# Decay attention with two expert layers: loads of 128 rows, and another order of the attention steps

## The chip, the cores and the metric

The kernel runs on 1 core of one Trainium2 chip. The metric is the device time of one execution in microseconds (us); smaller is better. Times are medians of several executions; one execution was also recorded by the profiler, and all rows below come from that one.

## The reference

Three parts follow each other. The first is a linear attention with a decay for each channel, over 4 batches, 8 heads, 768 steps and 48 channels a head:

```
for t in range(S):
    state = alpha[:, :, t, :, None] * state + einsum('bhd,bhe->bhde', k[:, :, t], v[:, :, t])
    y[:, :, t] = einsum('bhd,bhde->bhe', q[:, :, t], state)
```

Its output, as 3072 rows of 384, goes through a first expert layer (8 experts of 384 x 1024, one for each row, weighted by two gates) and a second one (8 experts, rows with a score of 0 or less skipped, the input added).

## The kernel before

The attention is worked in 24 chunks of 128 steps (`NTILE`), six for each batch. In a chunk, P is the running product of the decay; q is multiplied by P, k divided by it, and what is left is matmuls. Two heads share a tile: one on rows 0 to 47, the other on rows 64 to 111, so a tile of q, k or alpha has 112 rows (`PR`), of which rows 48 to 63 are padding. Three chunks make a half (`HB`), and a half is what a load brings; there are 8 halves. `ain`, `kin` and `qin` (alpha, k, q) have three buffers each, `vin` two.

A chunk i goes through these steps, each a function: `p_scan(i)` (DVE, L877) makes P. `p_recip(i)` (ACT, L886 and L887) makes r = 1/P as exp(-ln P). `p_q(i)` multiplies q by P (DVE, L915; ACT copies the chunk's last P into `ptots`, L919). `p_k(i)` makes the k product in three steps: t = P x r on POOL (L903; t has one buffer), then on DVE r = k x r (L904) and k2 = (2 - t) x r (L906), which corrects the reciprocal. `scores(i)` multiplies k2 by q on PE (L928), copies the result on ACT (L931) and masks it on POOL (L932, two AFFINE_SELECT). `k_back(i)` transposes k2 (PE L945, ACT L947). `state(i)` makes the state S after the chunk (PE L961 and L962, DVE L966 to L969); it reads v. `y_of(i)` makes the output (PE L980, L986; ACT L988), `x_rows(i)` turns it to rows (PE L269, ACT L274). `p_check(i)` (ACT, L893) tests alpha. Every fourth chunk closes a group of 512 tokens: `x_route` chooses experts (seven small DVE instructions, L147 to L246), `x_place` computes positions and sends the rows to memory with four indirect DMAs that POOL prepares (L218).

The order on every engine is the order in which the code issues the steps. A short written list (`lead`) starts the first chunks; then pass i of a loop calls the steps of the table `stages`, each with its lag: (p_scan, 4) in pass i is the scan of chunk i + 4. At the end of a pass come the DMAs of that pass. All of those loads go through SP's queue in that order: the halves (`load_half`), v (`load_v`), weight pieces of the first expert, and the fills, which write empty rows into the two scratch regions `scr1` (8 DMAs) and `scr2` (8 DMAs). For halves 3 to 7 `load_half` loads rows 0 to 47 and 64 to 111 with a DMA each, so that the padding stays; for the first three it loads all 112 rows. Some passes also split a weight piece into two parts (ACT L303, DVE L304).

Behind the attention come the two expert layers (`stream`), which begin with rows that the indirect DMAs of the attention's last full group but one have written.

Of the kernel before, what the change touches and what calls it, by code (L numbers as in the profile page):

```python
# [8 lines left out]
F32 = mybir.dt.float32  # L9
# [26 lines left out]
P1, G1 = 108, 4  # L36
# [8 lines left out]
FILL = 4  # L45
# [7 lines left out]
def kernel(  # L53
# [17 lines left out]
    nc = tc.nc  # L71
# [15 lines left out]
    scr1 = dp.tile([E * CAP + N1, PAY], F32, name="scr1")  # L87
# [759 lines left out]
    with ExitStack() as actx:  # L847
# [3 lines left out]
        ps1 = pool(actx, "ps1", 1, PSUM)  # L851
        NB_IN = 3
        NQ = 4
        ain = [inp.tile([128, HB, NP, C + 1], F32, name=f"ain{i}") for i in range(NB_IN)]
        kin = [inp.tile([128, HB, NP, C], F32, name=f"kin{i}") for i in range(NB_IN)]
        qin = [inp.tile([128, HB, NP, C], F32, name=f"qin{i}") for i in range(NB_IN)]
        vin = [inp.tile([128, HB, DM], F32, name=f"vin{i}") for i in range(2)]
        NHALF = 2 * B

        def load_half(h, which="akq", c0=0, c1=HB):  # L860
            s = h % NB_IN
            for r0, r1 in ((0, PR),) if h < NB_IN else ((0, 48), (64, PR)):
                for t in which:
                    dst, src = {"a": (ain[s], ad), "k": (kin[s], kd), "q": (qin[s], qd)}[t]
                    nc.sync.dma_start(out=dst[r0:r1, c0:c1], in_=src[h, r0:r1, c0:c1])

        def load_v(h):
            b, u = divmod(h, 2)
            nc.sync.dma_start(out=vin[h % 2], in_=vn[b][:, u * HB:(u + 1) * HB])

        P_t, r_t, k_t, q_t, A_t, kn_t, S_t, x_t, xt_t, sm_t, rt_t, lt_t = ({} for _ in range(12))

# [161 lines left out]
        def among(fn, i0, i1):  # L1034
            def run(i):
                if i0 <= i < i1:
                    fn(i)

            return run
# [1 line left out]
        rest = NTILE - GT * (LATE + 1)  # L1041
        x_route_0, x_place_0 = (among(fn, 0, rest) for fn in (x_route, x_place))
        x_route_1, x_place_1 = (among(fn, rest, NTILE) for fn in (x_route, x_place))
        p_q_0, p_q_1 = among(p_q, 0, NTILE - 1), among(p_q, NTILE - 1, NTILE)

        nbias = cp.tile([128, 1], F32, name="nbias")
        floor = cp.tile([128, NP, C + 1], F32, name="floor")
# [12 lines left out]
        for which, c in (("ak", 0), ("a", 1), ("q", 0), ("kq", 1), ("a", 2)):  # L1060
# [10 lines left out]
        w_cur = alloc_w(wpe, 0)  # L1071
        pieces = []
        stages = (
            (state, -1), (x_route_1, -3), (p_k, 2), (scores, 0), (k_back, 0), (x_place_0, -4), (x_place_1, -3),
            (x_route_0, -3), (p_recip, 3), (p_q_0, 2), (p_q_1, 1), (y_of, -1), (p_scan, 4), (x_rows, -2), (p_check, 0),
        )

        def constants(n):
# [2 lines left out]

        lead = (
            (p_scan, 0), (p_q, 0), (p_recip, 0), (p_scan, 1), (p_recip, 1), (p_k, 0), (p_q, 1), (scores, 0), (k_back, 0),
            (p_k, 1), (p_scan, 2), (p_recip, 2), (constants, FILL), (scores, 1), (k_back, 1),
            (p_q, 2), (p_scan, 3), (p_k, 2), (p_recip, 3), (state, 0), (y_of, 0), (scores, 2), (k_back, 2), (p_scan, 4),
        )
        for fn, i in lead:
            fn(i)
        done = lead + tuple((p_q_0, i) for fn, i in lead if fn is p_q)
        early_at = (NTILE // GT - LATE) * GT - 1 - dict(stages)[x_place_1]  # L1090
        for i in range(NTILE + 2):
            if i == early_at + 1:
                bump(ohs1, ecl1, sm_t[NTILE // GT - LATE - 1][0:1, 400:401], EARLY1)
            for fn, lag in stages:
                if 0 <= i + lag < NTILE and (fn, i + lag) not in done:
                    fn(i + lag)
                if fn is p_scan and 6 <= i < 24 and i % 3:
                    split_half(w_cur, (i - 6) // 3, i % 3 - 1, pieces[(i - 6) // 3])
            if i % HB == 1 and 2 <= (i + 2) // HB < NHALF:
                load_v((i + 2) // HB)  # L1100
            if i == early_at:
                xe = []
                for g0 in range(0, ITEMS[0][4], 2):
                    g1 = min(g0 + 2, ITEMS[0][4])
                    st = stp.tile([128, 1024], F32, name="st")
                    part = st[:, 0:(g1 - g0) * PAY].rearrange("p (g d) -> p g d", g=g1 - g0)
                    load_into(part, ITEMS[0], g0, g1)
                    xe += [part[:, g] for g in range(g1 - g0)]
            if i == 8:
                fill_region(scr2, P2, G2)  # L1110
            if i == HB:
                load_half(HB, "a")
                fill_region(scr1, P1, G1, FILL)
            if i >= HB and i % HB == 1 and i // HB + 2 < NHALF:
                load_half(i // HB + 2, "akq" if i > HB + 1 else "kq")
            if 4 <= i and i % 3 == 1 and (i - 4) // 3 < 6:
                pieces.append(load_piece(w1a, w2a, 0, (i - 4) // 3, stp))

# [102 lines left out]
def _lay_out(x):  # L1221
    import numpy as np

    q, k, v, a = (np.asarray(x[n]) for n in ("q", "k", "v", "alpha"))

    def d_major(t, pad):
        o = np.full((B, PR, NP, S), pad, t.dtype)
        r = t.reshape(B, NP, 2, S, D).transpose(2, 0, 4, 1, 3)
        o[:, 0:48] = r[0]
        o[:, 64:PR] = r[1]  # L1230
        return o

    def by_chunk(t, edge):
        o = np.zeros((2 * B, PR, HB, NP, C + edge), t.dtype)
        o[..., edge:] = t.reshape(B, PR, NP, 2, HB, C).transpose(0, 3, 1, 4, 2, 5).reshape(2 * B, PR, HB, NP, C)
        return o

    qm, km, am = d_major(q, 0), d_major(k, 0), d_major(a, 1)
    m = {"qd": by_chunk(qm, 0), "kd": by_chunk(km, 0), "ad": by_chunk(am, 1)}
    m["vn"] = v.reshape(B, H, NCH, C, D).transpose(0, 3, 2, 1, 4).reshape(B, C, NCH, DM)  # L1240
    m["akq"] = np.stack([am, km, qm]).transpose(4, 2, 0, 1, 3).reshape(S, PR, 3, B * NP)
    m["vtm"] = v.reshape(B, NP, 2, S, D).transpose(3, 2, 0, 1, 4).reshape(S, 2, B * NP, D)
    g1 = np.concatenate([np.asarray(x["moe_w_gate"]), np.asarray(x["moe_w_output_gate"])], axis=1)
    g2 = np.concatenate([np.asarray(x["moe2_w_gate"]), np.asarray(x["moe2_w_skip"])[:, None]], axis=1)
    gp = np.zeros((PR, NP, LW), g1.dtype)
    gr = g1.reshape(NP, 2, D, 2 * E).transpose(1, 2, 0, 3)
    gp[0:48, :, 0:2 * E] = gr[0]
    gp[64:PR, :, 0:2 * E] = gr[1]
    m["wg1"] = gp
    m["wg1k"] = g1.reshape(KB, 128, 2 * E).transpose(1, 0, 2)  # L1250
    m["wg2"] = np.zeros((128, KB, LW), g2.dtype)
    m["wg2"][:, :, 0:E + 1] = g2.reshape(KB, 128, E + 1).transpose(1, 0, 2)
    for s, n in (("a", "moe"), ("b", "moe2")):
        m["w1" + s] = np.asarray(x[n + "_w1"]).reshape(E, KB, 128, FF).transpose(0, 2, 1, 3)
        m["w2" + s] = np.asarray(x[n + "_w2"]).reshape(E, FB, 128, DM).transpose(0, 2, 1, 3)
    return {n: np.ascontiguousarray(m[n]) for n in _ARGS}
# [24 lines left out]
```

## Time and profile before

| | |
|---|---|
| executions (us) | 605.78, 607.69, 1037.39; median 607.69 |
| profiled execution | 607.02 us, of which the span of instructions is 605.3 |
| PE, DVE, ACT, POOL busy | 92%, 63%, 53%, 33% of the span |
| mean granted TensorE clock | 0.951 |
| DMA | 100.14 MB, mean 165 GB/s |

The profiled execution stands for the two fast ones (605.78 and 607.69); the third is left out of what follows. The busy shares are means over two very different stages, the attention and the expert layers, and must be read stage by stage.

### The profile page before, as it was taken

The page shows a single profiled execution, that of the slowest core. Times are in us where ns is not written, and L with a number is a line of the kernel's source. Part 1 is how long each engine was busy: PE and PEld are TensorE (multiplying, and loading weights), DVE is VectorE, ACT ScalarE, POOL GpSimd, SP SyncE. Part 2 cuts the span into 40 slices and gives each one's busy share as a digit, 9 for nine tenths or more (in the row PEclk, how much of TensorE's full clock was granted, in tenths as well). Part 3 has the DMA queues.
Part 4 walks back from the last instruction along what each step waited for, and adds up shares of the span by engine and source line. Part 5 has one row for each costly group of instructions (what it writes and reads, how often), then busy time and mean ns, then how long its engine had stood idle before and what let it go on. Part 6 is the DMA issues. An engine that isn't in the chain of part 4 may idle for free. (4 is left out here: it accounts for less than half of the span.)

```text
span 605.3 us, 11804 instructions
## 1 busy us (share of the span) xinstructions
PE 559.2 (92%) x4545; PEld 506.8 (84%) x4545; DVE 381.4 (63%) x846; ACT 319.2 (53%) x723; POOL 200.6 (33%) x210
## 2 busy tenths in 40 slices
PE   6994978779779999999999999999998999999995
PEld 5873767658659889999999999999997999999994
DVE  6896696979726446383746555554644876677851
ACT  3764765857654444454535444444444755565640
POOL 3853666575742041041322405060514011011111
PEclk9696897977999999999999999999999999999998
DMA  9989999592134814336261717162525566666620
GB/s 242 250 279 280 246 293 239 140 215 78 54 120 130 260 32 133 132 97 198 61 209 30 246 38 246 47 226 71 177 97 182 179 209 231 211 213 223 206 74 22
DMA packets 34318, 100.14 MB, mean 165 GB/s; under 512 B 6556, under 2 KB 13340, under 8 KB 34252
## 3 DMA queue, kind: packets, MB, share of 16 engines
q1 hardware_dynamic: 27308, 87.33, 49.2%
q0 software_dynamic: 6944, 11.96, 5.8%
q8 instruction: 38, 0.62, 0.4%
q14 instruction: 28, 0.23, 0.1%
HBM read 78.78 MB, written 27.13 MB: 175 GB/s over the span
## 5 line engine op out<-in xcount | busy, mean ns | idle before, releaser
L218 POOL DMA_INDIRECT scr<-x,pi x56 | 66.8, 1193 | 211.8 <-DVE osb L201 133.1
L399 PE MATMUL ph<-xh,w1h 128*128 128x432 f32 (+3 forms) x330 | 109.9, 333 | 0.0
L399 PE MATMUL ph<-xl,w1h 128*128 128x432 f32 (+3 forms) x330 | 106.3, 322 | 0.6 <-DVE xl L360 0.6
L399 PE MATMUL ph<-xh,w1l 128*128 128x432 f32 (+3 forms) x330 | 106.1, 322 | 0.0
L405 DVE SCALAR_TENSOR_TENSOR hl<-ph,hh 128x432 fp32r<-128x432 f32 (+3 forms) x110 | 56.2, 511 | 71.0 <-ACT hh L404 62.6
L404 ACT ACTIVATE hh<-ph 128x432 fp32r<-128x432 f32 (+3 forms) x110 | 50.1, 455 | 93.0 <-PE ph L399 83.4
L304 DVE TENSOR_TENSOR w2l<-st,w2h 128x512 fp32r<-128x512 f32 x96 | 64.4, 687 | 47.5 <-ACT w2h L303 40.1
L303 ACT ACTIVATE w2h<-st 128x512 fp32r<-128x512 f32 x96 | 58.1, 625 | 48.0 <-DMA st<-in_w2a_dram 26.8
L446 PE MATMUL py<-hh,w2h 128*128 128x432 f32 (+1 forms) x192 | 69.0, 359 | 0.0
L446 PE MATMUL py<-hh,w2l 128*128 128x432 f32 (+1 forms) x192 | 67.4, 351 | 0.0
L446 PE MATMUL py<-hl,w2h 128*128 128x432 f32 (+1 forms) x192 | 67.3, 351 | 0.0
L304 DVE TENSOR_TENSOR w1l<-st,w1h 128x512 fp32r<-128x512 f32 x96 | 63.0, 685 | 4.4 <-ACT w1h L303 2.3
L399 PEld LDWEIGHTS ph<-xh,w1h 128*128 128x128 f32 x330 | 62.4, 189 | 3.1 <-issue 1.6
L399 PEld LDWEIGHTS ph<-xl,w1h 128*128 128x128 f32 x330 | 62.2, 188 | 2.4 <-DVE xl L360 1.0
L399 PEld LDWEIGHTS ph<-xh,w1l 128*128 128x128 f32 x330 | 62.4, 189 | 1.2
L303 ACT ACTIVATE w1h<-st 128x512 fp32r<-128x512 f32 x96 | 56.5, 623 | 1.2 <-DMA st<-in_w1a_dram 1.2
L218 POOL DMA_INDIRECT out_dram<-ot,ti x16 | 15.6, 975 | 123.7 <-DVE ot L550 113.2
L932 POOL TENSOR_SCALAR_AFFINE_SELECT A<-A 128x512 f32<-128x512 f32 x48 | 46.0, 982 | 20.9 <-ACT A L931 20.8
L455 PE MATMUL py<-w2h,hh 128*128 128x384 f32 (+1 forms) x136 | 48.4, 356 | 0.0
L877 DVE TENSOR_TENSOR_SCAN P<-ain,floor 112x516 f32<-112x516 f32 x24 | 43.6, 1817 | 7.2 <-DMA ain<-in_ad_dram 7.2
L455 PE MATMUL py<-w2l,hh 128*128 128x384 f32 (+1 forms) x136 | 45.8, 337 | 0.0
L455 PE MATMUL py<-w2h,hl 128*128 128x384 f32 (+1 forms) x136 | 43.8, 337 | 0.0
(216 smaller groups left out, 1134.4 us busy)
## 6 DMA issues: line engine op xcount, KB each, us to landing
st<-in_w1a_dram SPq DMA_DIRECT2D x24, 512.0 KB
st<-in_w2a_dram SPq DMA_DIRECT2D x24, 512.0 KB
st<-in_w1b_dram SPq DMA_DIRECT2D x24, 512.0 KB
st<-in_w2b_dram SPq DMA_DIRECT2D x24, 512.0 KB
scr<-fill SPq DMA_DIRECT2D x8, 654.8 KB
vin<-in_vn_dram SPq DMA_DIRECT2D x8, 576.0 KB
xr<-scr SPq DMA_DIRECT2D x7, 654.8 KB
scr<-fill SPq DMA_DIRECT2D x8, 388.0 KB
```

What stands on the lines that cost most here:

```text
L218: ins = nc.gpsimd.indirect_dma_start(out=dst, out_offset=bass.IndirectOffsetOnAxis(ap=idx.bitcast(U32)[0:pp, j:j + 1], axis=0), in_=src, i ...
L303: nc.scalar.activation(out=hi, in_=src, func=AF.Copy)
L304: nc.vector.tensor_tensor(out=lo, in0=src, in1=hi.bitcast(F32), op=ALU.subtract)
L399: nc.tensor.matmul(ph[:, 0:n], w[:, kb, f * 128:(f + 1) * 128], x[:, kb, 0:n], start=(k == 0), stop=(k == 3 * KB - 1),)
L404: nc.scalar.activation(out=hh[:, f, 0:n], in_=ph[:, 0:n], func=AF.Relu)
L405: nc.vector.scalar_tensor_tensor(out=hl[:, f, 0:n], in0=ph[:, 0:n], scalar=0.0, in1=hh[:, f, 0:n].bitcast(F32), op0=ALU.max, op1=ALU.subtract,
L446: nc.tensor.matmul(py[d], w[:, f, dsl], hx[:, f, 0:pp * gg], start=(f == 0 and k == 0), stop=(f == FB - 1 and k == 2),)
L455: nc.tensor.matmul(py[g], hx[:, f, gsl], w[:, f, :], start=(f == 0 and k == 0), stop=(f == FB - 1 and k == 2),)
L877: nc.vector.tensor_tensor_scan(out=P.rearrange("p a b -> p (a b)"), data0=a[0:PR, c].rearrange("p a b -> p (a b)"), data1=floor[0:PR].rear ...
L932: nc.gpsimd.affine_select(out=a, in_=a, pattern=[[0, 4], [1, C]], base=0, channel_multiplier=-1, compare_op=ALU.is_ge, fill=0.0,)
```

## The change

Inputs: alpha, k and q are laid out with 128 rows in place of 112, rows 112 to 127 and 48 to 63 being padding, and `load_half` loads all 128 rows of a half with one DMA for each of the three. `vin` gets a third buffer.

Loads: half 3 is loaded in pass 2, before the fills of `scr1`, and every later half h in pass 3h - 7, three halves ahead. Before, alpha of half 3 was loaded in pass 3 and half h in pass 3h - 5. The fills of `scr2` move from pass 8 to pass 16.

Order: a pass now begins with `p_recip(i + 2)` and `p_q(i + 2)`, and the scan of chunk i + 3 stands behind `p_k(i + 2)`. Before, a pass had `p_recip(i + 3)` and `p_scan(i + 4)`. `p_check` goes two chunks ahead, the last chunk's own place for `p_q` goes, and `lead` is rewritten to fit.

```diff
-        vin = [inp.tile([128, HB, DM], F32, name=f"vin{i}") for i in range(2)]
+        vin = [inp.tile([128, HB, DM], F32, name=f"vin{i}") for i in range(NB_V)]
...
-            for r0, r1 in ((0, PR),) if h < NB_IN else ((0, 48), (64, PR)):
-                for t in which:
-                    dst, src = {"a": (ain[s], ad), "k": (kin[s], kd), "q": (qin[s], qd)}[t]
-                    nc.sync.dma_start(out=dst[r0:r1, c0:c1], in_=src[h, r0:r1, c0:c1])
+            for t in which:
+                dst, src = {"a": (ain[s], ad), "k": (kin[s], kd), "q": (qin[s], qd)}[t]
+                nc.sync.dma_start(out=dst[:, c0:c1], in_=src[h, :, c0:c1])
...
         stages = (
-            (state, -1), (x_route_1, -3), (p_k, 2), (scores, 0), (k_back, 0), (x_place_0, -4), (x_place_1, -3),
-            (x_route_0, -3), (p_recip, 3), (p_q_0, 2), (p_q_1, 1), (y_of, -1), (p_scan, 4), (x_rows, -2), (p_check, 0),
+            (p_recip, 2), (p_q, 2), (state, -1), (x_route_1, -3), (p_k, 2), (scores, 0), (k_back, 0), (x_place_0, -4),
+            (x_place_1, -3), (x_route_0, -3), (p_scan, 3), (y_of, -1), (x_rows, -2), (p_check, 2),
         )
...
-            if i == 8:
+            if i >= HB - 1 and i % HB == HB - 1 and i // HB + 3 < NHALF:
+                load_half(i // HB + 3, "akq")
+            if i == HB:
+                fill_region(scr1, P1, G1, FILL)
+            if i == 16:
                 fill_region(scr2, P2, G2)
-            if i == HB:
-                load_half(HB, "a")
-                fill_region(scr1, P1, G1, FILL)
-            if i >= HB and i % HB == 1 and i // HB + 2 < NHALF:
-                load_half(i // HB + 2, "akq" if i > HB + 1 else "kq")
...
-        o = np.zeros((2 * B, PR, HB, NP, C + edge), t.dtype)
-        o[..., edge:] = t.reshape(B, PR, NP, 2, HB, C).transpose(0, 3, 1, 4, 2, 5).reshape(2 * B, PR, HB, NP, C)
+        o = np.zeros((2 * B, 128, HB, NP, C + edge), t.dtype)
+        o[:, 0:PR, ..., edge:] = t.reshape(B, PR, NP, 2, HB, C).transpose(0, 3, 1, 4, 2, 5).reshape(2 * B, PR, HB, NP, C)
```

DVE before, from the q product in pass 7 to the k product in pass 8 (`P_653` is P of chunk 9, `P_857` of chunk 11; `k2_894` is the k product of chunk 10):

```order
L915 TENSOR_TENSOR qp_843<-qin0_119,P_653 112x512
L877 SCALAR_TENSOR_TENSOR P_857<-ain0_113,floor_125 112x516
L304 TENSOR_TENSOR w1l0_191<-st_593,w1h0_190 128x512
L968 TENSOR_TENSOR S_888<-pu_879,S_773 112x192
L969 TENSOR_TENSOR S_888<-S_888,ptots_95 112x192
L904 TENSOR_TENSOR r_840<-kin0_116,r_840 112x512
L906 SCALAR_TENSOR_TENSOR k2_894<-t_891,r_840 112x512
```

The scan here is of the chunk behind the one whose k product follows. The same place now (`P_846` is P of chunk 10, `P_919` of chunk 11):

```order
L877 SCALAR_TENSOR_TENSOR P_846<-ain0_113,floor_126 112x516
L304 TENSOR_TENSOR w1l0_192<-st_590,w1h0_191 128x512
L915 TENSOR_TENSOR qp_876<-qin0_119,P_846 112x512
L968 TENSOR_TENSOR S_888<-pu_879,S_779 112x192
L969 TENSOR_TENSOR S_888<-S_888,ptots_95 112x192
L904 TENSOR_TENSOR r_873<-kin0_116,r_873 112x512
L906 SCALAR_TENSOR_TENSOR k2_894<-t_891,r_873 112x512
L877 SCALAR_TENSOR_TENSOR P_919<-ain0_113,floor_126 112x516
```

Now the scan and the k product behind it are of the same chunk, and the next chunk's scan stands behind that k product.

ACT before, in pass 8 (`P_857` is P of chunk 11, `xt_942` the output of chunk 7):

```order
L931 ACTIVATE A_906<-ps_896 128x512
L931 ACTIVATE A_909<-ps_897 128x512
L947 ACTIVATE kn_917<-pk_912 128x448
L886 ACTIVATE r_919<-P_857 112x512
L887 ACTIVATE r_919<-r_919 112x512
L919 ACTIVATE ptots_95<-P_751 112x4
L988 ACTIVATE xt_942<-py_925 112x512
```

ACT now, from the end of pass 7 into pass 8 (`P_846` is P of chunk 10):

```order
L988 ACTIVATE xt_859<-py_850 112x512
L274 ACTIVATE x2_753<-pxt_861 128x4x48 x2
L893 ACTIVATE junk_868,relus_96<-ain0_113,nbias_125 112x516
L886 ACTIVATE r_873<-P_846 112x512
L887 ACTIVATE r_873<-r_873 112x512
L919 ACTIVATE ptots_95<-P_846 112x4
L931 ACTIVATE A_906<-ps_896 128x512
```

The reciprocal of pass 8 is of chunk 10 in place of chunk 11, and it stands ahead of the copies of the scores.

## Rows read from the trace of the kernel before

**Rows 1.** Busy time by stretch: attention, then expert layers (engines, clock, DMA share, GB/s)

```profile
0.00:183.75 183.75, 148.97 (x1858) 119.53 (x1858) 137.99 (x236) 116.78 (x291) 108.82 (x126) 0.85 0.76 201
183.75:605.30 421.55, 410.18 (x2692) 387.25 (x2688) 243.43 (x610) 202.42 (x432) 91.81 (x84) 0.99 0.47 150
```

**Rows 2.** Timeline, DVE: k products (start, us) of eleven chunks

```profile
28.69 0.69 DVE L906 SCALAR_TENSOR_TENSOR k<-t,r 112x512 f32<-112x512 f32 x1
...
50.51 0.69 DVE L906 SCALAR_TENSOR_TENSOR k<-t,r 112x512 f32<-112x512 f32 x1 [0.52 <-DVE r L904]
...
62.99 1.00 DVE L906 SCALAR_TENSOR_TENSOR k<-t,r 112x512 f32<-112x512 f32 x1
...
73.30 1.00 DVE L906 SCALAR_TENSOR_TENSOR k<-t,r 112x512 f32<-112x512 f32 x1
...
84.71 0.69 DVE L906 SCALAR_TENSOR_TENSOR k<-t,r 112x512 f32<-112x512 f32 x1
...
103.07 1.00 DVE L906 SCALAR_TENSOR_TENSOR k<-t,r 112x512 f32<-112x512 f32 x1
...
113.93 0.69 DVE L906 SCALAR_TENSOR_TENSOR k<-t,r 112x512 f32<-112x512 f32 x1
...
130.36 1.00 DVE L906 SCALAR_TENSOR_TENSOR k<-t,r 112x512 f32<-112x512 f32 x1
...
141.62 0.93 DVE L906 SCALAR_TENSOR_TENSOR k<-t,r 112x512 f32<-112x512 f32 x1
...
158.01 1.00 DVE L906 SCALAR_TENSOR_TENSOR k<-t,r 112x512 f32<-112x512 f32 x1
...
162.57 1.00 DVE L906 SCALAR_TENSOR_TENSOR k<-t,r 112x512 f32<-112x512 f32 x1
```

**Rows 3.** Timeline, PE and DVE: the waits for loads at 52 to 62 us

```profile
57.95 0.31 PE L961 MATMUL pu<-vin,kn 128*64 128x48 f32 x1 [6.62 <-DMA vin<-in_vn_dram]
...
61.88 1.07 DVE L904 TENSOR_TENSOR r<-kin,r 112x512 f32<-112x512 f32 x1 [2.46 <-DMA kin<-in_kd_dram]
```

**Rows 4.** Busy time by stretch: 112-row loads, v, 48-row loads, v and weights

```profile
14.00:20.00 6.00, 5.43 (x52) 4.54 (x51) 5.31 (x7) 4.59 (x10) 5.57 (x14) 0.50 1.01 238
120.50:121.50 1.00, 1.00 (x17) 0.88 (x17) 0.96 (x3) 1.00 (x4) 0.00 (x0) 1.00 1.05 430
123.00:132.00 9.00, 5.19 (x68) 4.14 (x67) 4.73 (x8) 4.91 (x12) 7.35 (x8) 0.86 1.02 153
```

**Rows 5.** Timeline, SP: the first four fills of scr1

```profile
21.93 9.87 SPq L139 DMA_DIRECT2D scr<-fill  x4
```

**Rows 6.** Timeline, first loads: DVE and POOL waiting

```profile
6.16 1.23 DVE L877 TENSOR_TENSOR_SCAN P<-ain,floor 112x516 f32<-112x516 f32 x1 [1.11 <-DMA ain<-in_ad_dram]
...
7.11 1.26 POOL L915 TENSOR_TENSOR qp<-qin,P 112x512 f32<-112x512 f32 x1 [5.72 <-DMA qin<-in_qd_dram]
```

**Rows 7.** Timeline, DVE, ACT and POOL: scan, reciprocal, t, masks, k product

```profile
72.17 1.10 DVE L904 TENSOR_TENSOR r<-kin,r 112x512 f32<-112x512 f32 x1 [3.99 <-POOL t L903]
...
74.83 2.23 DVE L877 TENSOR_TENSOR_SCAN P<-ain,floor 112x516 f32<-112x516 f32 x1
...
98.03 1.23 DVE L877 TENSOR_TENSOR_SCAN P<-ain,floor 112x516 f32<-112x516 f32 x1 [3.35 <-DMA ain<-in_ad_dram]
...
99.96 0.63 ACT L887 ACTIVATE r<-r 112x512 f32<-112x512 f32 x1
...
65.19 1.67 POOL L218 DMA_INDIRECT scr<-x,pi  x1 [1.74 <-DVE osa L201]
...
70.92 1.21 POOL L903 TENSOR_TENSOR t<-P,r 112x512 f32<-112x512 f32 x1
72.05 1.70 POOL L932 TENSOR_SCALAR_AFFINE_SELECT A<-A 128x512 f32<-128x512 f32 x2
```

**Rows 8.** Timeline, DVE: first of the seven routing instructions, and what follows them

```profile
85.32 0.18 DVE L147 TENSOR_REDUCE mxa<-smp 128x4 f32<-128x32 f32 x1
...
87.62 1.12 DVE L915 TENSOR_TENSOR qp<-qin,P 112x512 f32<-112x512 f32 x1
```

More of the change, by code (lines that the diff above doesn't have):

```diff
@@ L853 @@
         NQ = 4
+        NB_V = 3
         ain = [inp.tile([128, HB, NP, C + 1], F32, name=f"ain{i}") for i in range(NB_IN)]
@@ L861, in load_half @@
             s = h % NB_IN
-            for r0, r1 in ((0, PR),) if h < NB_IN else ((0, 48), (64, PR)):
-                for t in which:
-                    dst, src = {"a": (ain[s], ad), "k": (kin[s], kd), "q": (qin[s], qd)}[t]
-                    nc.sync.dma_start(out=dst[r0:r1, c0:c1], in_=src[h, r0:r1, c0:c1])
+            for t in which:
+                dst, src = {"a": (ain[s], ad), "k": (kin[s], kd), "q": (qin[s], qd)}[t]
+                nc.sync.dma_start(out=dst[:, c0:c1], in_=src[h, :, c0:c1])
         def load_v(h):
             b, u = divmod(h, 2)
-            nc.sync.dma_start(out=vin[h % 2], in_=vn[b][:, u * HB:(u + 1) * HB])
+            nc.sync.dma_start(out=vin[h % NB_V], in_=vn[b][:, u * HB:(u + 1) * HB])
         P_t, r_t, k_t, q_t, A_t, kn_t, S_t, x_t, xt_t, sm_t, rt_t, lt_t = ({} for _ in range(12))
@@ L950, in v_of @@
         def v_of(i):
-            return vin[(i // HB) % 2][:, i % HB]
+            return vin[(i // HB) % NB_V][:, i % HB]
         def state(i):
@@ L1043 @@
         x_route_1, x_place_1 = (among(fn, rest, NTILE) for fn in (x_route, x_place))
-        p_q_0, p_q_1 = among(p_q, 0, NTILE - 1), among(p_q, NTILE - 1, NTILE)
         nbias = cp.tile([128, 1], F32, name="nbias")
@@ L1083 @@
             (p_scan, 0), (p_q, 0), (p_recip, 0), (p_scan, 1), (p_recip, 1), (p_k, 0), (p_q, 1), (scores, 0), (k_back, 0),
-            (p_k, 1), (p_scan, 2), (p_recip, 2), (constants, FILL), (scores, 1), (k_back, 1),
-            (p_q, 2), (p_scan, 3), (p_k, 2), (p_recip, 3), (state, 0), (y_of, 0), (scores, 2), (k_back, 2), (p_scan, 4),
+            (p_k, 1), (p_check, 0), (p_check, 1), (p_scan, 2), (p_recip, 2), (constants, FILL), (scores, 1), (k_back, 1),
+            (p_q, 2), (p_k, 2), (p_check, 2), (state, 0), (p_scan, 3), (y_of, 0), (scores, 2), (k_back, 2),
         )
@@ L1088 @@
             fn(i)
-        done = lead + tuple((p_q_0, i) for fn, i in lead if fn is p_q)
+        done = lead
         early_at = (NTILE // GT - LATE) * GT - 1 - dict(stages)[x_place_1]
```

## The prediction

> **What bounds the kernel now.** I read the stretches first, then the k products one by one, then what stood in front of the long ones.
>
> The expert layers take 421.55 us with TensorE busy for 410.18 [rows 1]. The change doesn't touch them, so what matters is by how much their begin, at 183.75 us, moves.
>
> In the attention no engine is full (PE 148.97, DVE 137.99, ACT 116.78, POOL 108.82 of 183.75 us) and the DMA is busy for 0.76 of it [rows 1]. So I measure it by the start of the last DVE step of a chunk, the k product. From chunk 4 (28.69) to chunk 23 (162.57) it takes 133.88 us for 19 chunks [rows 2]. They are of two kinds. Eleven plain intervals (28.69 to 50.51, 73.30 to 84.71, 103.07 to 113.93, 130.36 to 141.62, 158.01 to 162.57) sum to 59.91, 5.45 each. Four pairs hold a routing and then the placing of a group: 22.79, 18.36, 16.43 and 16.39, together 73.97. The first pair is long because of loads: PE waits 6.62 us for v until 57.95 and DVE then 2.46 us for k until 61.88 [rows 3]. The other three average 17.06, so the loads cost 22.79 - 17.06 = 5.7 us there. The 3.35 us for alpha at 98.03 [rows 7] I count as nothing: in such a pass POOL is preparing four indirect DMAs, and t stands behind them; in the first pair the four go from 65.19 to 70.92, and DVE waits 3.99 us for t [rows 7].
>
> **Faster loads.** What removes the wait at 57.95 is the rate. While loads of 48 rows are in flight, all 16 DMA engines are busy and move 153 GB/s; loads of 112 rows make 238; v, which has 128 rows, goes at 430 [rows 4]. So 128 rows are cheaper although they carry more: a half is then 774 + 768 + 768 = 2310 KB (the shapes of the diff), 5.5 us at 430 GB/s, against 11.6 us for its 96 rows at 153. The Trainium skill, "DMA: Bandwidth & Descriptors", section "Why a DMA increments its semaphore by 16 and not by 1", says that a DMA takes the largest number of engines up to 16 that divides its slowest dimension. By that rule 48 and 112 rows get all 16 engines as well, and the padding would only add bytes; the rows of the trace agree that all engines are busy, but not that the rates are equal.
>
> When v of half 2 arrives: ahead of it in SP's queue stand four halves (9.46 MB, 22 us at 430), v of halves 0 to 2 itself included (1.77 MB, 4.1 us) and eight fills, 9.87 / 4 = 2.47 us each [rows 5], 19.7 us. From 2 us on, that is 48 us. By the ring below, the k product of chunk 8 is at 28.69 - 1.1 + 4 x 5.94 = 51.4; routing (2.30) and a scan (1.23) stand between it and the state step that needs v, so it is wanted at about 55. The wait is gone: -5.7 us. It would come back if the halves moved at less than 325 GB/s (9.46 MB in the 29 us that are left).
>
> The very first loads are also in the way: DVE waits 1.11 us for alpha of chunk 1, and POOL multiplies q of chunk 0 only from 7.11 [rows 6]. With 8/7 of the bytes at the old rate that becomes 1.0 later, at 430 GB/s 2.6 earlier (7.11 x (1 - 8/7 x 238/430)). I take -1.1, the wait itself, because from there on POOL's constants, which are not moved, set the pace up to chunk 4.
>
> **The order.** This takes time back. Before, the scan was two steps ahead: its reciprocal, and then t, had a whole pass each. Now the steps of one chunk form a ring: the scan of chunk i + 3 stands on DVE behind the k product of i + 2; its reciprocal on ACT, then t on POOL, then the k product on DVE must follow before the next scan may start. Round it, from rows 7: scan begin to reciprocal end 98.03 to 99.96 + 0.63 = 2.56; t begin to the first step behind it 70.92 to 72.17 = 1.25; from there to the k product 72.17 to 73.30 = 1.13 [rows 2]; the k product 1.00 [rows 2]. Sum 5.94 us for a plain interval. The q product, the state and the weight split fit on DVE while it waits for the reciprocal and t, so they are hidden (if the ring were shorter than they are, they would cost their own time, as before). The two masks lie between these steps: POOL runs them right behind t (72.05, 1.70 us for two), which is why 1.10 and 1.00 stand there [rows 7, 2].
>
> Bounds of the ring: if the masks came too late to meet the k product, that takes 0.69 as at 84.71 [rows 2] and the step ahead of it, by my estimate, as much, and the ring is 2.56 + 1.25 + 0.69 + 0.69 = 5.2. If the scan meets them, it takes 2.23 as at 74.83 in place of 1.23 [rows 7], and the ring is 6.94. I take 5.94, since rows 7 show t, masks and k product in just the order that the new table gives.
>
> Routing stands between the k product and the scan, so it adds its 87.62 - 85.32 = 2.30 us [rows 8]: 8.24. Placing is then followed by the four indirect DMAs on POOL, t behind them, and the k product. That chain is the same in both orders, and longer than the ring, so I keep 73.30 - 62.99 = 10.31 [rows 2]. A pair is 18.55.
>
> Sum: 11 x 5.94 = 65.3 against 59.9, +5.4. Four pairs 74.2 against 74.0, +0.2: the wait for loads in the first pays for the routing of all four. The first loads -1.1. Together +4.5, and the profiled execution's 607.02 us becomes 611.5; the median is 0.67 above it, so 612.
>
> **What I cost at nothing.** The third v buffer frees SP from waiting for the output of chunk 2. `p_check` is moved, not added; it now stands on ACT right ahead of the next reciprocal, and ACT, with 116.78 / 24 = 4.9 us a chunk [rows 1], has room in 5.94. Each half's loads now wait on SP for the checks, k and q products of the half three before, with v and weight pieces queued behind them; those are done two passes earlier. The later fills of `scr2` are covered by the first expert layer; if they got in front of what is needed, they would cost at most their queue time, some 10 us. From chunk 23 on, the placing, the indirect DMAs and the first rows follow as before.
>
> **Rivals.** *The order is free.* Then only the loads count: -5.7 - 1.1 gives 600.2, 601 against the median. For it speaks that POOL's and DVE's steps already take turns: the scan is 1.23 us alone and 2.23 beside POOL [rows 7], so shortening one wait may only move another. The Trainium skill, "SBUF — State Buffer", section "SBUF: two separate sides", calls the port pair of the two engines an exclusive lock held for a whole instruction, which agrees with 72.05 to 74.30, where they alternate; by that rule the sum of both engines' work, the same in either order, would be the floor. Against it: in the new ring DVE and POOL both stand idle while ACT makes the reciprocal.
>
> *The padded loads are no faster,* as the rule on 16 engines has it. Four halves at 238 GB/s take 39.8 us in place of 22; v of half 2 lands at 65.6 in place of 57.95, and the k product of chunk 9, some 2 us behind it, moves from 62.99 to 67.6, +4.6. Behind it come seven plain intervals, 41.6 against 38.1, and three pairs, 55.7 against 51.2: +8.0 more. That is 619.6, 620 against the median: slower. It decides at the 325 GB/s above. At 153 GB/s it would be 22 us worse still.
>
> *The ring is longer.* PE is busy for 148.97 / 24 = 6.2 us a chunk [rows 1], and ACT's copies of the previous pass, which wait for PE, now stand ahead of the reciprocal. Where PE or the scan beside the masks holds the ring up to 6.94, the eleven plain and four routing intervals cost 1.0 more each: up to 627.
>
> **How the numbers follow.** The ring about as worked out, 606 to 617: 0.56. Order free, 598 to 603: 0.18. Loads no faster, 618 or more: 0.10. Longer ring, 617 to 627: 0.10. What is left, 0.06, is between these or below. The range 600 to 620 leaves out the upper ends of the two slow cases and the lower part of the free order, about 0.2. A measurement can tell 2% from no change, 12 us; faster by that (under 595.5) needs a ring under 5.2 and more: 0.04; slower (over 619.8): 0.13; within: 0.83.
>
> **What would show it.** Right: no wait of PE for v near 58, GB/s over 400 while halves load; k products 5.9 apart in plain passes, DVE waiting for POOL's t in nearly every one, the scan at 1.23 us; routing intervals of 8.2; the expert layers' begin near 188. Wrong: plain intervals of 5.5 or less, or waits for loads that come back. Most likely to upset it is the 0.49 us by which I make a plain pass longer: it is counted 15 times.

## The result and the profile after

The changed kernel takes 615.83 us (median of 11 executions, 610.77 to 617.93), the kernel before 609.08 beside it (median of 11). The ratio is 1.0107, with a 95% interval of 1.0069 to 1.0145: slower by 6.5 us, which is under the 2% and inside the range, 3.8 us above the predicted time. Executions more than 1.5% above the fastest one of their kernel are not counted in the ratios, here one of 1037.39 us of the kernel before, below three of "changed, scan one further" and one of the kernel before.

The recorded execution of the changed kernel took 617.36 us, 1.5 above its median; that of before took 607.02, 2.1 below the median that it has now. So the two traces differ by 10.3 us, and 3.6 of it are the choice of executions. Busy time by stretch, attention and then expert layers, in the trace after (columns as in [rows 1]):

```profile
0.00:193.97 193.97, 155.30 (x1858) 125.04 (x1858) 132.49 (x236) 116.27 (x291) 100.30 (x126) 0.81 0.59 210
193.97:615.60 421.63, 411.51 (x2692) 388.11 (x2688) 243.26 (x610) 202.52 (x432) 93.46 (x84) 0.99 0.46 150
```

The expert layers take 421.63 us (421.55 in [rows 1]), so all of the difference lies ahead of them: they begin at 193.97 in place of 183.75. DVE and POOL are less busy than before and the stretch is longer: what grew on them is waiting.

One turn of the attention, chunk 6 to chunk 7, in the timelines of DVE, ACT and POOL of the trace after:

```profile
41.95 1.00 DVE L906 SCALAR_TENSOR_TENSOR k<-t,r 112x512 f32<-112x512 f32 x1
42.88 1.22 DVE L877 TENSOR_TENSOR_SCAN P<-ain,floor 112x516 f32<-112x516 f32 x1
...
46.79 1.10 DVE L904 TENSOR_TENSOR r<-kin,r 112x512 f32<-112x512 f32 x1 [1.23 <-POOL t L903]
47.92 1.00 DVE L906 SCALAR_TENSOR_TENSOR k<-t,r 112x512 f32<-112x512 f32 x1
...
44.13 0.63 ACT L886 ACTIVATE r<-P 112x512 f32<-112x512 f32 x1 [1.53 <-DVE P L877]
44.80 0.63 ACT L887 ACTIVATE r<-r 112x512 f32<-112x512 f32 x1
...
45.56 1.19 POOL L903 TENSOR_TENSOR t<-P,r 112x512 f32<-112x512 f32 x1 [3.15 <-DVE S L969]
46.69 1.69 POOL L932 TENSOR_SCALAR_AFFINE_SELECT A<-A 128x512 f32<-128x512 f32 x2
```

Read it as a ring: the k product at 41.95, the scan behind it, the reciprocal on ACT as soon as the scan ends (1.53 us of waiting), t on POOL as soon as the reciprocal ends, DVE waiting for t, the next k product. POOL's releaser is given as the state on DVE, which ends as t begins (45.56). It is the reciprocal for which t waits: it ends at 45.43, 0.13 us ahead of t, and with the longer reciprocal below t begins 0.14 us behind it as well, though the state was done 0.66 us earlier. The parts are 0.93 to the scan, 2.68 to t, 1.23 to the step behind it and 1.13 to the k product: 5.97 us. The same waits, summed over 20 to 175 us (us, times, longest):

```profile
ACT r L886 <- DVE P L877: 52.2, 20, 5.4
DVE r L904 <- POOL t L903: 33.8, 14, 5.4
```

Over the same stretch before, ACT waited 21.0 us for P (10 times) and DVE 15.4 for t (5 times).

The k products of chunks 4, 8, 9, 10 and 23, DVE's timeline of the trace after, which answer to [rows 2]:

```profile
30.36 0.69 DVE L906 SCALAR_TENSOR_TENSOR k<-t,r 112x512 f32<-112x512 f32 x1
...
53.88 1.00 DVE L906 SCALAR_TENSOR_TENSOR k<-t,r 112x512 f32<-112x512 f32 x1
...
61.27 1.00 DVE L906 SCALAR_TENSOR_TENSOR k<-t,r 112x512 f32<-112x512 f32 x1
...
72.49 1.00 DVE L906 SCALAR_TENSOR_TENSOR k<-t,r 112x512 f32<-112x512 f32 x1
...
169.77 1.00 DVE L906 SCALAR_TENSOR_TENSOR k<-t,r 112x512 f32<-112x512 f32 x1
```

With [rows 1, 2] all but 0.1 of the 10.3 us split into three: chunk 4 comes at 30.36 in place of 28.69, +1.67; from chunk 4 to chunk 23 it takes 139.41 in place of 133.88, +5.53; from there to the expert layers 24.20 in place of 21.18, +3.02. The middle one is what the prediction worked out (+5.4 and +0.2).

### The profile page after: what moved, and what is told of

It is laid out like the page before. It is cut to its first block, busy times and chain, and to the rows that moved or that the text cites. A ratio compares the mean times of both kernels' runs of the same rounds, so it can differ in the third digit from the quotient of the medians.

```text
span 615.6 us, 11780 instructions
## 1 busy us (share of the span) xinstructions
PE 566.8 (92%) x4545; PEld 513.1 (83%) x4545; DVE 375.8 (61%) x846; ACT 318.8 (52%) x723; POOL 193.8 (31%) x210
## 4 chain that ended last, share of the span: by engine, by line
PE 61%; DMA 7%; DVE 4%; POOL 2%; ACT 2%; issue 2%; POOLq 0%; SPq 0%; ACTq 0%; DVEq 0%
PE ph L399 25%; PE py L446 16%; PE py L455 7%; PE py L399 3%; DMA st<-in_w2b_dram 3%; PE pt L355 2%; DMA st<-in_w2a_dram 2%; PE pt L485 2%; PE ph L417 1%; POOL scr L218 1%; PE smp L475 1%; DMA st<-scr 1%; DVE P L877 1%; POOL t L903 1%; DVE r L904 1%
## 5 line engine op out<-in xcount | busy, mean ns | idle before, releaser
L904 DVE TENSOR_TENSOR r<-kin,r 112x512 f32<-112x512 f32 x24 | 25.6, 1067 | 34.0 <-POOL t L903 33.8
L980 PE MATMUL py<-A,vin 128*48 128x128 f32 (+1 forms) x384 | 36.3, 329 | 8.6 <-POOL A L932 8.6
## 6 DMA issues: line engine op xcount, KB each, us to landing
scr<-fill SPq DMA_DIRECT2D x8, 654.8 KB
```

Source lines behind the costliest of these rows:

```text
L904: nc.vector.tensor_tensor(out=r, in0=kk, in1=r, op=ALU.mult)
L980: nc.tensor.matmul(py[m0:m1, hp], v[:, v0:v0 + w], at[j][:, hp], start=(hp == 0 or c == 0), stop=(c == 0))
```

## The experiments

The changed kernel ran first, the others in three groups of four, each beside the kernel before on the same chip; the ratios are to that. The times in us behind a ratio in the text are that part of 609.08.

| kernel | us | ratio to before | 95% interval |
|---|---|---|---|
| changed kernel | 615.83 | 1.0107 | 1.0069 to 1.0145 |
| new loads, order of before | 603.13 | 0.9903 | 0.9869 to 0.9937 |
| the same, another group | 602.53 | 0.9879 | 0.9843 to 0.9916 |
| new order, loads of before | 617.83 | 1.0142 | 1.0088 to 1.0197 |
| changed, longer reciprocal | 625.69 | 1.0262 | 1.0204 to 1.0319 |
| before, longer reciprocal | 609.84 | 0.9998 | 0.9957 to 1.0039 |
| padding only | 604.63 | 0.9869 | 0.9811 to 0.9926 |
| new loads, t early | 598.48 | 0.9770 | 0.9714 to 0.9825 |
| changed, scan one further | 608.17 | 0.9929 | 0.9889 to 0.9968 |
| new loads, v early | 604.22 | 0.9845 | 0.9787 to 0.9903 |
| changed, loads by rows | 621.05 | 1.0185 | 1.0143 to 1.0228 |
| new loads, t and v early | 591.49 | 0.9714 | 0.9665 to 0.9763 |
| changed, lead of before | 612.55 | 1.0051 | 1.0021 to 1.0081 |

**The two halves of the change.** My theory: the loads give some 6.8 us and the new order takes more than that back. The main rival: the order is free.

The new loads, with the stages of before (in them only the check's lag is the new one):

```diff
             (state, -1), (x_route_1, -3), (p_k, 2), (scores, 0), (k_back, 0), (x_place_0, -4), (x_place_1, -3),
-            (x_route_0, -3), (p_recip, 3), (p_q_0, 2), (p_q_1, 1), (y_of, -1), (p_scan, 4), (x_rows, -2), (p_check, 0),
+            (x_route_0, -3), (p_recip, 3), (p_q_0, 2), (p_q_1, 1), (y_of, -1), (p_scan, 4), (x_rows, -2), (p_check, 2),
```

> The new loads (128 rows, three halves ahead, ahead of the fills, third v buffer) with the order of before (scan four chunks ahead, reciprocal three ahead, q product as before; the checks stay two chunks ahead). If the order is a ring that costs time and the loads only gain: the plain intervals between k products go back to about 5.45 us, no wait for v or k near 60 us, the expert layers begin some 6 us earlier than before, and the time is 602 to 604 (ratio 0.990 to before). If the order were free and the loss came from the loads (more bytes, later fills): 615 as with the whole change.

> The new loads with the order of before once more, beside kernels with a shorter attention. In the kernels of the last group the expert layers took 429 to 431 us, with one on another chip 424.9. If that comes from the chip: this one's expert layers take about 429 to 431 us here too. If it comes from an earlier begin of the expert layers: 424 to 426 us here, and more only in the kernel with t and v early. The first pair holds a wait for v near 57 us either way, since v stands behind half 3 and the fills.

The new order and its `lead`, with the loads of before:

```diff
-            (state, -1), (x_route_1, -3), (p_k, 2), (scores, 0), (k_back, 0), (x_place_0, -4), (x_place_1, -3),
-            (x_route_0, -3), (p_recip, 3), (p_q_0, 2), (p_q_1, 1), (y_of, -1), (p_scan, 4), (x_rows, -2), (p_check, 0),
+            (p_recip, 2), (p_q, 2), (state, -1), (x_route_1, -3), (p_k, 2), (scores, 0), (k_back, 0), (x_place_0, -4),
+            (x_place_1, -3), (x_route_0, -3), (p_scan, 3), (y_of, -1), (x_rows, -2), (p_check, 2),
```

> The new order with the loads of before (112 rows, then 48 and 48, two v buffers, fills where they were). If the ring costs the time: plain intervals of 5.96 us, and the wait for the loads of half 3 near 60 us still there but partly covered by the slower passes, so the k product of chunk 9 at 63 us in place of 61.3; 616 to 619 us, a little above the whole change. If the order is free: 609 as before.

The loads alone gave 0.97% and 1.21%, that is 5.9 and 7.4 us; the order alone cost 1.42%, 8.6 us; the order on top of the new loads cost 13 us (615.83 against 603.13 and 602.53). The order is not free. (In both halves the check is two chunks ahead; no run tests that step by itself.) The parts don't add: beside the new order the loads are worth 0.35%, 2.1 us, with overlapping intervals. In the two traces the first pair takes 18.61 us with the new loads and 22.96 without them, where DVE waits 6.89 us for q and the k product of chunk 9 comes at 66.74, not at the 63 expected; but from chunk 23 to the expert layers it is 24.20 against 22.31.

The gain of the loads is not the gain that I described. PE's timeline of the new loads with the order of before:

```profile
57.30 0.31 PE L961 MATMUL pu<-vin,kn 128*64 128x48 f32 x1 [5.55 <-DMA vin<-in_vn_dram]
```

The wait for v is still there, 0.65 us earlier than in [rows 3], and from chunk 8 to chunk 10 it takes 21.92 us (22.79 before). The second time this kernel ran, v came at 55.35 after a wait of 4.81. What its recorded executions did gain lies in several places: k products of chunks 4 to 23 in 131.17 and 130.23 us against 133.88; the interval with the wait for alpha at 98.03 [rows 7], now gone, fell from 10.87 to 10.00 us. The first of them begins its expert layers at 183.73, no earlier than the kernel before and not the 6 us earlier that I expected; the second at 180.56. So these two traces show only a part of the 5.9 and 7.4 us.

**The ring.** A copy of the reciprocal by itself on ACT, one instruction of 0.63 us that changes no value, makes the reciprocal longer. It was put into the changed kernel and into the kernel before:

```diff
+            nc.scalar.activation(out=r, in_=r, func=AF.Copy)
```

> The whole change with one more instruction in the reciprocal: ACT copies r onto itself behind the exponential (some 0.65 us more on ACT for each chunk; results unchanged). If scan, reciprocal, t and k product are a ring, each of the 15 plain and routing intervals grows by the whole 0.65, to 6.6 and 8.1 us, and the placing ones, where t waits for the indirect DMAs, not at all: +10 to +12 us, 626 to 628. If POOL and DVE together set the pace (the port they share), ACT's extra instruction is hidden: 616.

> The kernel before with the same extra copy of r on ACT. In that order the reciprocal has a pass of slack, so the 0.65 us is not on the way: 609 to 612, up to 3 us only where ACT itself gets full (it works some 5 us of 5.45 in a plain pass). If the reciprocal were on the way before as well, +10 as with the change: 619.

One turn of the changed kernel with the copy, from k product to k product, DVE's timeline (L907 there is L906):

```profile
44.41 1.00 DVE L907 SCALAR_TENSOR_TENSOR k<-t,r 112x512 f32<-112x512 f32 x1
...
51.03 1.00 DVE L907 SCALAR_TENSOR_TENSOR k<-t,r 112x512 f32<-112x512 f32 x1
```

The turn grew from 5.97 to 6.62 us, by the whole of the copy, routing intervals to 8.1, placing intervals not at all, and the kernel by 1.55%, 9.4 us (10 to 12 expected). In the order of before the same copy, as often, cost nothing. So ACT's reciprocal lies in the ring after, and beside other work before. The copy is work for ACT alone, so that the interval grew by it also speaks against the work of DVE and POOL together setting the pace. The second way to open the ring is to give the scan a pass more:

```diff
-            (x_place_1, -3), (x_route_0, -3), (p_scan, 3), (y_of, -1), (x_rows, -2), (p_check, 2),
+            (x_place_1, -3), (x_route_0, -3), (p_scan, 4), (y_of, -1), (x_rows, -2), (p_check, 2),
...
-            (p_q, 2), (p_k, 2), (p_check, 2), (state, 0), (p_scan, 3), (y_of, 0), (scores, 2), (k_back, 2),
+            (p_q, 2), (p_k, 2), (p_check, 2), (state, 0), (p_scan, 3), (y_of, 0), (scores, 2), (k_back, 2), (p_scan, 4),
```

> The changed kernel with the scan one chunk further ahead (chunk i + 4 in place of i + 3 at the same place in the pass); the reciprocal, the q product and the loads stay as changed. If the ring closes through the scan (scan, reciprocal, t, k product, next scan): plain intervals fall from 5.96 to 5.0 to 5.5 us, and the time to 602 to 606 us. If the place of the reciprocal and of the q product at the head of the pass holds it: 614 to 617 us, plain intervals of 5.9.

A turn of that kernel, DVE's timeline:

```profile
75.38 0.69 DVE L906 SCALAR_TENSOR_TENSOR k<-t,r 112x512 f32<-112x512 f32 x1
75.99 1.22 DVE L877 TENSOR_TENSOR_SCAN P<-ain,floor 112x516 f32<-112x516 f32 x1
77.14 1.62 DVE L915 TENSOR_TENSOR qp<-qin,P 112x512 f32<-112x512 f32 x1
...
79.39 1.11 DVE L904 TENSOR_TENSOR r<-kin,r 112x512 f32<-112x512 f32 x1
80.53 0.69 DVE L906 SCALAR_TENSOR_TENSOR k<-t,r 112x512 f32<-112x512 f32 x1
```

The turn takes 5.15 us, DVE waits for nothing in it, and the kernel is 1.78% (10.8 us) below the changed one. That is most of the 13 us. 608.17 is above the 606 that I expected, in a group in which the kernel before took 611.38. The eleven plain intervals average 5.51 us, at the upper end of what I gave. The scan's distance closed the ring, with little left for the place of the reciprocal.

**The rate of the loads.** Padding and one DMA for each load, at the load times and in the order of before:

```diff
-            for r0, r1 in ((0, PR),) if h < NB_IN else ((0, 48), (64, PR)):
-                for t in which:
-                    dst, src = {"a": (ain[s], ad), "k": (kin[s], kd), "q": (qin[s], qd)}[t]
-                    nc.sync.dma_start(out=dst[r0:r1, c0:c1], in_=src[h, r0:r1, c0:c1])
+            for t in which:
+                dst, src = {"a": (ain[s], ad), "k": (kin[s], kd), "q": (qin[s], qd)}[t]
+                nc.sync.dma_start(out=dst[:, c0:c1], in_=src[h, :, c0:c1])
```

> Only the layout of 128 rows and the single DMA for each load; the loads' times, the two buffers of v and the order are those of before. If the rate of the loads alone makes the gain of the new loads: 600 to 605 us, and no wait of PE for v near 58 us (only alpha of half 3 and not the whole half stands ahead of it in SP's queue). If the earlier load times make it: 608 to 611 us, with the wait for v or k still there.

And the reverse: the changed kernel, in which these lines are put back.

> The changed kernel, its order, load times and v buffers kept, with the loads of alpha, k and q by rows as before: 112 rows for the first three halves, then rows 0 to 47 and 64 to 111 with a DMA each. If the rate of 128-row loads is worth something in the new order: v of half 2 lands at 62 to 66 us in place of 54.5, the k product of chunk 9 comes at 64 to 68 in place of 61.3, and the time is 618 to 624 us. If earlier load times alone would have done, or the ring hides the loads: 614 to 617 us.

The padding alone gives 1.31%, 8.0 us: all of what the new loads give; that the earlier load times and the third v buffer add to it doesn't show. The time is as expected; that the wait for v would go is not what came: v landed at 53.37 after a wait of 4.94. Still, its first pair is 4.4 us shorter than before (18.44 against 22.79), most of the 5.7 that the prediction gave to the loads there:

```profile
49.25 0.69 DVE L905 SCALAR_TENSOR_TENSOR k<-t,r 112x512 f32<-112x512 f32 x1
...
67.69 1.00 DVE L905 SCALAR_TENSOR_TENSOR k<-t,r 112x512 f32<-112x512 f32 x1
```

In the new loads with the order of before v came later, at 57.30 and 55.35: there the whole of half 3 stands ahead of it in SP's queue, here only its alpha. Without the padding the changed kernel loses 0.78%, 4.7 us, with intervals that just touch. Stretches of that kernel and, below it, of the changed one (columns as in [rows 1]):

```profile
5.00:15.00 10.00, 5.16 (x42) 4.21 (x39) 7.93 (x8) 3.53 (x8) 2.98 (x3) 0.82 1.06 264
55.00:65.00 10.00, 0.00 (x0) 0.00 (x0) 4.91 (x11) 2.88 (x8) 3.10 (x4) 0.54 1.03 260
118.00:122.00 4.00, 3.60 (x61) 3.04 (x59) 3.71 (x4) 3.17 (x9) 1.84 (x3) 1.00 1.05 168
```

```profile
5.00:15.00 10.00, 6.14 (x53) 5.16 (x52) 8.70 (x9) 4.87 (x11) 4.51 (x4) 0.84 1.03 392
55.00:65.00 10.00, 10.00 (x103) 8.38 (x101) 7.95 (x22) 5.59 (x15) 3.14 (x4) 0.60 1.02 422
```

All DMA engines are busy in the five stretches. In the first ones, where the loads of all 112 rows go, the rates are 264 and 392 GB/s. From 55 to 65 the loads of 48 rows are a small part: SP issues v at 51.59, a weight piece at 55.19 and the first of them at 56.46, and fills are still in flight; 260 is the rate of that mixture, 422 that of halves, v and weights with the padding. The loads of 48 rows by themselves show from 118 to 122 us, with all that SP had issued since 110 being such loads, v behind them and the next fills: 168 GB/s, near the 153 of [rows 4]. By rows, PE waits 14.58 us for v, until 67.62, and does nothing from 55 to 65; the k product of chunk 9 comes at 69.73, both a little later than expected. The rule that I weighed in the prediction (the Trainium skill, "DMA: Bandwidth & Descriptors", section "Why a DMA increments its semaphore by 16 and not by 1") is right about the engines, as far as these shares tell, and leaves the rate open.

**The waits that stay.** Two edits on the new loads with the order of before. First, v of half 2 ahead of half 3 and of the fills:

```diff
-            if i % HB == 1 and 2 <= (i + 2) // HB < NHALF:
+            if i % HB == 1 and 3 <= (i + 2) // HB < NHALF:
                 load_v((i + 2) // HB)
...
+            if i == HB - 1:
+                load_v(2)
```

> The new loads with the order of before, and v of half 2 issued in pass 2, ahead of half 3 and of the fills of scr1. If the wait of PE for v until 57.30 us is on the path: the first pair falls from 21.92 to about 16.7 us, the mean of the other three in that kernel, and the time by some 5 us, to 597 to 599 us. If the pair is held by something else that comes as late: 602 to 604 us.

Second, t moved in the table from the k product to just behind the reciprocal, a whole pass earlier and ahead of the indirect DMAs (`p_t` holds the line of t):

```diff
-            (state, -1), (x_route_1, -3), (p_k, 2), (scores, 0), (k_back, 0), (x_place_0, -4), (x_place_1, -3),
-            (x_route_0, -3), (p_recip, 3), (p_q_0, 2), (p_q_1, 1), (y_of, -1), (p_scan, 4), (x_rows, -2), (p_check, 2),
+            (state, -1), (x_route_1, -3), (p_k, 2), (scores, 0), (k_back, 0), (p_recip, 3), (p_t, 3),
+            (x_place_0, -4), (x_place_1, -3), (x_route_0, -3), (p_q_0, 2), (p_q_1, 1), (y_of, -1), (p_scan, 4), (x_rows, -2), (p_check, 2),
```

> The new loads with the order of before, and t of a chunk moved on POOL right behind its reciprocal, ahead of the indirect DMAs. If t behind the four indirect DMAs is what makes the placing intervals 10 us long: DVE's waits of about 4 us for t go, the placing intervals fall to 6 to 7 us, and the time to 588 to 595 us. If another step holds the placing interval (the indirect DMAs push the masks, or DVE's own work): within 3 us of the 603 us of the new loads with the order of before.

> The new loads with the order of before, t right behind the reciprocal, and v of half 2 ahead of half 3 and of the fills: both of the single edits together. If the two waits are separate, the gains in the attention add: the k products of chunks 4 to 23 take 117 to 119 us (131.17 with neither, 126.63 with v alone, 121.77 with t alone), and the time is 3 to 5 us below t alone, 594 to 596 us. If one hides the other: 598 us.

With v early, the k products of chunks 8, 9 and 10, DVE's timeline:

```profile
49.56 0.69 DVE L906 SCALAR_TENSOR_TENSOR k<-t,r 112x512 f32<-112x512 f32 x1
...
55.74 0.69 DVE L906 SCALAR_TENSOR_TENSOR k<-t,r 112x512 f32<-112x512 f32 x1
...
64.60 1.10 DVE L904 TENSOR_TENSOR r<-kin,r 112x512 f32<-112x512 f32 x1 [3.99 <-POOL t L903]
65.74 1.01 DVE L906 SCALAR_TENSOR_TENSOR k<-t,r 112x512 f32<-112x512 f32 x1
```

The pair takes 16.18 us in place of 21.92: the wait is worth 5.7 us, the number that I took from the four pairs of the kernel before. The time fell less: 0.34% to 0.58% (2 to 3.5 us) below the new loads alone, with overlapping intervals, 604.22 in place of the 597 to 599 expected. The recorded executions of that group tell a part of this: in its four kernels the expert layers took 425.0 to 426.7 us, in all other kernels 418.8 to 421.8 (the expectation of the repeated run counts them from some 4 us earlier, at their first transposes). The new loads alone, on another chip, took 420.6 there, and so did the kernel with t and v early (421.3), whose expert layers begin earliest, at 168.70. So the earlier begin is not what lengthens them; it came with that group.

With t early, a pair and the interval behind it, DVE's timeline (L915 there is L906, L913 is L904):

```profile
87.84 0.69 DVE L915 SCALAR_TENSOR_TENSOR k<-t,r 112x512 f32<-112x512 f32 x1
...
93.39 0.69 DVE L915 SCALAR_TENSOR_TENSOR k<-t,r 112x512 f32<-112x512 f32 x1
...
99.02 1.10 DVE L913 TENSOR_TENSOR r<-kin,r 112x512 f32<-112x512 f32 x1 [2.95 <-POOL t L904]
100.16 1.00 DVE L915 SCALAR_TENSOR_TENSOR k<-t,r 112x512 f32<-112x512 f32 x1
```

The placing interval falls from 10.00 to 5.55 us, but the next one grows from 4.76 to 6.77: behind the four indirect DMAs POOL now has masks and t in a row, and DVE waits 2.95 us for that t. So 2.0 of the 4.5 us came back, and the kernel reached 598.48, not 588 to 595. Both edits together add: chunks 4 to 23 take 116.98 us (117 to 119 expected), the time is 591.49 (594 to 596 expected), 2.9% below the kernel before and, by the two ratios, 3.9% below the changed one. It beats both.

**The lead.** The changed kernel with the scan and the reciprocal of chunk 3 back in their places:

```diff
-            (p_q, 2), (p_k, 2), (p_check, 2), (state, 0), (p_scan, 3), (y_of, 0), (scores, 2), (k_back, 2),
+            (p_q, 2), (p_scan, 3), (p_k, 2), (p_recip, 3), (p_check, 2), (state, 0), (y_of, 0), (scores, 2), (k_back, 2),
```

> The changed kernel with the scan and the reciprocal of chunk 3 put back into the written list ahead of chunk 2's k product, as before. If the ring already sets the pace in the first chunks: the k product of chunk 3 comes near 22.6 us in place of 25.18, that of chunk 4 near 28.6 in place of 30.36, and the time falls by 1.7 us, to about 614. If POOL's constants set the pace up to chunk 4: the k product of chunk 4 stays near 30 us.

DVE's timeline of the changed kernel at the k product of chunk 3, with t on DVE, and below it that of this kernel, chunks 3 and 4:

```profile
23.34 0.76 DVE L903 TENSOR_TENSOR t<-P,r 112x512 f32<-112x512 f32 x1 [1.96 <-ACT r L887]
24.14 1.00 DVE L904 TENSOR_TENSOR r<-kin,r 112x512 f32<-112x512 f32 x1
25.18 0.69 DVE L906 SCALAR_TENSOR_TENSOR k<-t,r 112x512 f32<-112x512 f32 x1
```

```profile
21.08 1.01 DVE L906 SCALAR_TENSOR_TENSOR k<-t,r 112x512 f32<-112x512 f32 x1
...
27.14 0.69 DVE L906 SCALAR_TENSOR_TENSOR k<-t,r 112x512 f32<-112x512 f32 x1
```

Chunk 4 comes 3.22 us earlier (30.36 to 27.14), more than the 1.7 expected, and the time falls by 0.56%, 3.4 us, to 612.55. In the changed kernel the ring holds the lead too, and POOL's constants don't: POOL is done with them and with four masks at 24.60 and then stands 3.82 us until its t. With the lead of before the constants do set the pace: masks and t follow them without a gap. POOL's timeline of the changed kernel and, below it, of this one:

```profile
28.41 1.18 POOL L903 TENSOR_TENSOR t<-P,r 112x512 f32<-112x512 f32 x1 [3.82 <-DVE S L969]
```

```profile
20.86 4.27 POOL L932 TENSOR_SCALAR_AFFINE_SELECT A<-A 128x512 f32<-128x512 f32 x4
25.10 1.28 POOL L903 TENSOR_TENSOR t<-P,r 112x512 f32<-112x512 f32 x1
```

## Why the prediction held, and where its terms did not

**The ring: right, in mechanism and size.** The eleven plain intervals sum to 65.70 us against 65.3 forecast (59.91 before); a turn is 5.97 against 5.94, and the scan is at 1.22. The copy on ACT and the scan one chunk further show that the reciprocal and the scan's distance hold it. The longer ring of the third rival did not come: the four longest plain intervals are 6.08.

**The four pairs: right as a sum, by two errors that cancel.** They take 73.71 us against 74.2. Routing intervals took 7.39 to 7.52 in place of 8.24: its seven instructions take 1.43 us (54.81 to 56.24), not 2.30, since at 85.76 before one of them met POOL's t (85.58, 1.18 us) and took 1.04 in place of 0.19. Placing intervals took 10.56 to 11.22 in place of 10.31. "That chain is the same in both orders" was wrong by 0.7 us in the mean: DVE's scan now stands right behind the positions. In the first pair the first indirect DMA begins as the scan ends; in the other three it begins 0.2 us behind the positions and takes 2.65, 2.01 and 2.65 us beside the scan, where the same three took 1.53 before. POOL's timeline after, in the first two pairs:

```profile
64.67 1.60 POOL L218 DMA_INDIRECT scr<-x,pi  x1 [2.93 <-DVE P L877]
...
94.21 2.65 POOL L218 DMA_INDIRECT scr<-x,pi  x1 [1.72 <-DVE osa L201]
```

In the first row, DVE's step on which it waited before (L201) ends at 63.27, 1.40 us earlier; before, it began 0.2 us behind the end of that step. The Trainium skill, "SBUF — State Buffer", section "SBUF: two separate sides", has DVE and GpSimd lock a shared port pair for a whole instruction, with which this row agrees.

**The wait for v: right that it leaves the path, wrong about when v comes.** After, PE waits 3.45 us for v until 54.50; the k product of chunk 9 has no wait of loads in its chain:

```profile
54.50 0.31 PE L961 MATMUL pu<-vin,kn 128*64 128x48 f32 x1 [3.45 <-DMA vin<-in_vn_dram]
```

I had v land at 48. The fills moved as I had them (272 GB/s from 26 to 28 us; 654.8 KB in 2.47 us is 271), and that the first of them waits on SP for POOL's constants, until 21.31, left no gap: from 20 to 24 us the DMA engines are busy for 1.00 of the time. What failed is the rate of the rest, which I had at 430 GB/s throughout: it was 165 in the first 5 us and 377 to 415 from there to 20, and while fills and half 3 go by turns, from 24 to 34 us, 293 at a share of 0.90. SP issued v at 40.78. The margin that remained is thin: with the earlier lead v at 55.17 makes PE wait 7.34 us, and the first pair takes 19.74 us in place of 18.61.

**The first loads: wrong, the step that failed.** I took -1.1 us "because from there on POOL's constants, which are not moved, set the pace up to chunk 4". Chunk 4 came 1.67 us later. DVE's first wait for alpha is 1.12 us as before: in the first 5 us the rate is 165 GB/s (160 before). And in the new lead it is the ring that sets the pace, not POOL's constants, which costs 3.2 us. With the lead of before chunk 4 comes at 27.14, 1.55 earlier than at [rows 2], but that is not the gain that I forecast for the loads: with the order of before the new loads bring it at 28.77 and 28.28, near the 28.69 of [rows 2]. What gives the rest of the 1.55 was not followed. The recorded execution is 5.9 us above the 611.5 worked out for it; this step is 2.8 of them, and the end of the attention 3.0. The median is 3.8 above the predicted one, and 1.4 of these are the kernel before's own: its median is 609.08 now and was 607.69 where I worked from it.

**The end of the attention: not foreseen.** From chunk 23's k product to the expert layers the recorded execution took 3.0 us more. At its begin the granted clock is on the lower of its two levels (0.50, 1.2 GHz), after two stretches in which PE was busy for 1.53 and 2.57 us of 3. Stretches of 3 us of the changed kernel and, below them, one of the kernel before, which ends as far ahead of its chunk 23 as the second one:

```profile
160.77:163.77 3.00, 1.53 (x18) 0.96 (x14) 1.18 (x2) 0.17 (x2) 3.00 (x4) 1.00 0.29 108
163.77:166.77 3.00, 2.57 (x30) 2.17 (x30) 3.00 (x4) 0.87 (x2) 0.37 (x1) 0.77 0.00 0
166.77:169.77 3.00, 3.00 (x41) 2.09 (x38) 2.93 (x4) 2.83 (x8) 2.47 (x3) 0.50 0.03 5
169.77:172.77 3.00, 3.00 (x35) 2.69 (x33) 2.69 (x9) 1.21 (x4) 0.46 (x1) 0.50 0.00 0
172.77:175.77 3.00, 3.00 (x28) 2.42 (x26) 1.43 (x10) 2.13 (x5) 1.23 (x2) 0.50 0.01 3
```

```profile
156.57:159.57 3.00, 1.48 (x18) 1.05 (x19) 2.66 (x4) 1.23 (x3) 2.28 (x4) 1.00 0.04 17
```

There PE was less busy, and the clock stayed at 1.00, so why it fell in the changed kernel is open. Sixteen matmuls of the scores take 2.08 us at the lower clock (at 171.15) and 1.16 in the trace before (at 162.93), and the indirect DMAs, which wait for such matmuls by way of the positions, begin 6.23 us behind the k product in place of 4.53, which is 1.7 of the 3.0 us. This doesn't belong to the order alone: the new order with the loads of before has the clock at 1.00 from 176.73 to 179.73, 3 us behind its last k product, and takes 22.3 us (196.04 less 173.73); the order of before with the new loads has it at 0.50 from 156.94 to 159.94, just ahead of its own, and takes 23.8 (183.73 less 159.94). But the changed kernel with the lead of before took 24.2 again, and the second execution of the order of before with the new loads 22.1. What the stretch adds to the median was not tested.

**The rivals.** That the order is free falls: its 601 us is what the loads alone give (603.13 and 602.53). That padded loads are no faster falls by their rates; its forecast of 620 us for the changed kernel with slow loads met 621.05.

## What to carry to other kernels

When a step that starts a chain over several engines is moved closer to its use, add up the chain from its begin to the end of the instruction behind which the next begin stands: where that sum is longer than the work of any engine in a turn, it is the new interval, whatever the busy shares are, and one extra stage of distance (here the scan one chunk further) takes most of it away again. The same sum must be made for the written-out first passes, which have an order of their own. A load lands behind what stands ahead of it in its queue (here the fills and a whole half), so add that up at the rates that the trace shows, and move the one small load that is needed first.

## What the runs showed of the hardware that was not expected

- The first loads, of 112 rows, kept all DMA engines busy and moved 264 GB/s; in 128 rows, a seventh more bytes, they moved 392. Loads of 48 rows moved 168, with the engines as busy. The padding alone was worth 1.31% of the kernel.
- A copy of 112 x 512 on ACT (0.63 us) in each chunk, 24 times, left the kernel before at a ratio of 0.9998 and made the changed kernel 1.55% longer.
- In one group of four kernels, on one chip, the expert layers took 425.0 to 426.7 us, and 418.8 to 421.8 in all the others, with the same code; in the two that I followed, the granted clock fell to 0.91 and 0.83 in a stretch of 20 us at the change from the first layer to the second, where the kernel before has 1.00. The kernel before took 611.38 us there and 609.77 and 609.43 beside the other groups, 1.6 to 2.0 less, so it shows at most a part of that. Whether that chip or something else made it is open.
